# A linear-attention and gated feed-forward kernel: instruction order from a list schedule made at build time, weights transposed by DMA at the start, five banks instead of three for keys, queries and values

## The chip, the cores and the metric

The kernel runs on one core of one Trainium2 chip. The metric is the device time of one execution in microseconds (us). The kernel before takes 217.75 us, the median of its runs. Executions of one kernel differ by about 1%, and some fall into a slower state. Spans quoted from a profile are those of the one execution that was profiled (216.6 us for the kernel before), which is a little shorter than the timed median.

## The reference

One token matrix x (2048 tokens, 512 channels) is layer-normed once. The normed tokens xn feed an attention with 32 heads of 16 channels without a softmax over tokens, and a gated feed-forward block of width 1376; x and both results are added.

```python
xn = layernorm(x)                                   # 2048 x 512
q, k, v = split(xn @ wqkv)                          # 32 heads of 16
pq, pk = q @ w_phi, k @ w_phi                       # per head, 16 x 16
phi_q = concat(softmax(pq), softmax(-pq))           # over 16 features
phi_k = concat(softmax(pk), softmax(-pk))
kv  = einsum("sf,sd->fd", phi_k, v)                 # summed over ALL tokens
num = phi_q @ kv;  den = phi_q @ sum_s(phi_k) + 1e-6
att = (num / den) @ wo
ffn = (gelu(xn @ w_gate) * (xn @ w_up)) @ w_down
out = x + att + ffn
```

Two things matter for the order of work. The attention of any token needs kv, the sum over all 16 token tiles of 128, so all keys and values come before the first attention output. The feed-forward block needs only xn and its weights.

## The kernel before

The weight w_phi is folded into the key and query weights at the start ("fold", 16 small matmuls each), so a key tile is one product of four 512-column matmuls, followed by two exponentials on ScalarE (for +pk and -pk) and four additions on GpSimd, which sum each group of 16 features. Products are written to banks: buffers that each hold one product until other engines have read it. A value tile is one product; VectorE scales it by the reciprocals of the key sums (`vs`), and TensorE accumulates keys times scaled values (`kv_acc`). The feed-forward stage begins when keys and queries are done.

Every instruction stands in the queue of its engine in the order in which the program was written by hand. A helper only adds the semaphore waits. The order of VectorE and GpSimd is therefore fixed by such code:

```python
def ln_rstd(t, n):                                   # VectorE adds, GpSimd takes the power -0.5
    op("dve", ... tensor_scalar(vpe, mv[.., 1], 1e-5, None, op0=ALU.add))
    op("pool", ... tensor_tensor(rstd, vpe, neghalf, op=ALU.pow))

def xt_dma(t):                                       # a normed tile is transposed by a DMA of SyncE
    dma("sp", ... dma_start_transpose(xnT[:, :, t * P:(t + 1) * P], xn_sb[:, t % NXN, :]))

# ---- start: x tile by tile on SyncE's queue, weights on ScalarE's queue, wq transposed by DMA, wk by TensorE
dma("act", ... wk_nat, A_wqkv[:, 512:1024]);  load_x(1)
dma("act", ... wv_sb,  A_wqkv[:, 1024:1536])
...
dma("sp",  ... dma_start_transpose(wqT, A_wqkv[:, 0:512]))
...
# 16 transposes of wk on TensorE, two copies (ScalarE, VectorE), then the folds, then:
for t in range(4, 8): ln_stats(t)
ln_rstd(4, 4)
proj_k(0, 0); proj_k(1, 1)
for t in range(4, 8): ln_norm(t); xt_dma(t)
proj_k(2, 0)
v_recip(0); v_scale(0, 4)                            # values 0 are scaled only here
...
# ---- middle: 28 units (12 keys, 16 queries) in two banks; values always in bank 4
for u, un in enumerate(units):
    b = u % 2
    ...                                              # layer norms of later tiles at fixed units
    if un[0] == "k": proj_k(un[1], b)
    else:            proj_q(un[1], un[2], b)
    ...
    if u % 3 == 2 and nbig < 5:                      # one big weight load every third unit
        big_loads(nbig); nbig += 1                   # wg, wu, wo, wd, tail of wd: on GpSimd's queue
```

The five big loads bring the weights of the later stage (1376, 1376, 512, 1280 and 96 KB). They are issued by GpSimd. They pass the issue points only when GpSimd gets there, because they stand in its queue between the key sums.

The softmax here doesn't subtract the row's maximum and nothing guards it: scores larger than these inputs give would overflow.

## Time and profile before

| quantity, kernel before | us |
|---|---|
| median time | 217.75 |
| span of the profiled execution | 216.6 |
| first key product starts | 14.54 |
| TensorE waits for scaled values, two waits | 6.6 |
| first gate/up product starts | 66.46 |
| from there to 213.50: TensorE busy | 145.26 of 147.04 |

The page of a profile shows in its second part the busy share of each engine in 40 equal slices of the span: each digit is tenths, 9 meaning 90% or more. PEclk is the clock granted to TensorE, in tenths of full speed. These lines are from the page of the kernel before; one slice is 5.4 us.

```profile
span 216.6 us, 3003 instructions
...
PE   7776399949999999999999999999999999998994
...
PEclk9999969997999999999999999999999999999999
...
```

TensorE is at 9 tenths from the tenth slice on, and nearly without a gap from 66 us on. What can be gained lies before that: the first four slices show 6 and 7 tenths, the fifth 3 and the ninth 4. The next lines are from the view of waits of TensorE: the engine and the line that waited, what it waited for, then total us, number of waits, and the longest.

```profile
...
PE ps_all L444 <- DVE vs L428: 6.6, 2, 3.5
...
PE ps_all L562 <- ACT y_sb L580: 0.8, 1, 0.8
...
```

L444 is the accumulation, L428 the scaling of a value tile on VectorE. The two waits end at 26.96 and at 46.94 us. The chain of waits of 6 to 30 us (start, duration, what) shows what stands before the first of them:

```profile
...
16.10 1.03 POOL rstd L345
17.15 2.89 DVE xn_sb L351 x4
20.04 0.48 DVE vs L422
20.55 1.23 DVE vs L428
21.77 0.61 DVE stats L336
...
25.18 0.48 DVE vs L422
25.68 1.24 DVE vs L428
26.96 0.76 PE ps_all L444 x8
...
```

The wait that ends at 26.96 us is for value tile 1. Its product was long done, and GpSimd had the key sums that its scaling needs ready at 22.71 us, but VectorE first takes the statistics of four other tiles (to 24.97 us). Before the second wait VectorE stands still for 2.6 us, for the rstd that GpSimd computes behind key sums. Just after each of the two waits, of 3.5 and 3.0 us, the granted clock falls to half for 3.4 us (from 27.36 and from 47.84 us), and matmuls run at half speed.

One more view: the timeline of GpSimd, cut to its issues of the five big loads (start, duration, line, tiles).

```profile
...
34.71 0.97 POOL L670 DMA_DIRECT2D wg_sb<-in_B_w_gate_dram  x1
...
38.48 0.77 POOL L673 DMA_DIRECT2D wu_sb<-in_B_w_up_dram  x1
...
45.80 0.78 POOL L676 DMA_DIRECT2D wo_sb<-in_A_wo_dram  x1
...
49.36 0.98 POOL L679 DMA_DIRECT2D wd_sb<-in_B_w_down_dram  x1
...
55.88 0.55 POOL L683 DMA_DIRECT2D wd_sb<-in_B_w_down_dram  x1
...
```

The transposes of xn tiles by DMA take 2.4 to 2.5 us to land when no load is in flight; the six that meet one or two loads take 3.2, 4.5, 2.5, 5.0, 3.0 and 6.5 us.

### The profile page before, as it was taken

The page shows a single profiled execution, that of the slowest core. Times are in us where ns is not written, and L with a number is a line of the kernel's source. Part 1 is how long each engine was busy: PE and PEld are TensorE (multiplying, and loading weights), DVE is VectorE, ACT ScalarE, POOL GpSimd, SP SyncE. Part 2 cuts the span into 40 slices and gives each one's busy share as a digit, 9 for nine tenths or more (in the row PEclk, how much of TensorE's full clock was granted, in tenths as well). Part 3 has the DMA queues.
Part 4 walks back from the last instruction along what each step waited for, and adds up shares of the span by engine and source line. Part 5 has one row for each costly group of instructions (what it writes and reads, how often), then busy time and mean ns, then how long its engine had stood idle before and what let it go on. Part 6 is the DMA issues. An engine that isn't in the chain of part 4 may idle for free.

```text
span 216.6 us, 3003 instructions
## 1 busy us (share of the span) xinstructions
PE 199.5 (92%) x1094; PEld 98.3 (45%) x1115; DVE 134.0 (62%) x302; ACT 75.8 (35%) x133; POOL 83.9 (39%) x114
## 2 busy tenths in 40 slices
PE   7776399949999999999999999999999999998994
PEld 2433154424444554554444455544455444543441
DVE  4698988593335877799459575494744777622121
ACT  2449537836886222232312313232232231422000
POOL 3219999999994000022424124323323222440200
PEclk9999969997999999999999999999999999999999
DMA  6892216969300000002020112101140111110101
GB/s 155 250 267 61 49 24 109 390 203 229 123 0 3 0 0 0 3 0 48 24 52 25 24 48 50 26 24 24 48 51 0 50 48 27 48 24 24 47 29 48
DMA packets 24590, 14.40 MB, mean 66 GB/s; under 512 B 18464, under 2 KB 23584, under 8 KB 24576
## 3 DMA queue, kind: packets, MB, share of 16 engines
q1 hardware_dynamic: 21920, 8.39, 17.0%
q0 software_dynamic: 1072, 4.75, 6.6%
q10 hardware_dynamic: 1584, 1.07, 1.8%
q8 instruction: 9, 0.15, 0.3%
q14 instruction: 5, 0.04, 0.1%
HBM read 7.91 MB, written 2.10 MB: 46 GB/s over the span
## 4 chain that ended last, share of the span: by engine, by line
PE 78%; DVE 13%; DMA 3%; POOL 2%; issue 2%; ACT 1%; ACTq 0%; DVEq 0%
PE ps_all L472 32%; PE ps_all L567 18%; PE ps_all L562 6%; PE ps_all L399 5%; PE ps_all L412 5%; PE ps_all L375 4%; PE ps_all L493 4%; PE ps_all L444 4%; DVE stats L336 3%; DMA hT<-in_A_wqkv_dram 3%; DVE xn_sb L351 2%; DVE vs L428 2%; POOL rstd L345 1%; DVE otmp L539 1%; DVE mv L338 1%
## 5 line engine op out<-in xcount | busy, mean ns | idle before, releaser
L485 DVE TENSOR_TENSOR hT<-gs,ps_all 128x512 bf16<-128x512 bf16 (+1 forms) x44 | 30.1, 683 | 31.9 <-PE ps_all L493 23.2
L482 ACT ACTIVATE gs<-ps_all 128x512 bf16<-128x512 f32 (+1 forms) x44 | 26.2, 597 | 57.0 <-PE ps_all L472 47.0
L472 PE MATMUL ps_all<-xnT,wg_sb 128*128 128x512 bf16 (+1 forms) x175 | 45.1, 379 | 0.1
L472 PE MATMUL ps_all<-xnT,wu_sb 128*128 128x512 bf16 (+1 forms) x170 | 44.5, 379 | 0.3
L567 PE MATMUL ps_all<-wd_sb,hT 128*128 128x512 bf16 (+1 forms) x171 | 40.4, 379 | 0.3
L551 POOL TENSOR_TENSOR o_sb<-otmp 128x512 bf16<-128x512 bf16 x16 | 18.4, 1152 | 54.6 <-DVE otmp L539 54.6
L582 POOL TENSOR_TENSOR ob<-y_sb,x_all 128x512 bf16<-128x512 f32 x12 | 13.8, 1153 | 47.3 <-ACT y_sb L580 47.3
L428 DVE TENSOR_TENSOR vs<-ps_all,vs 128x1024 bf16<-128x1024 f32 x16 | 19.6, 1227 | 14.2 <-PE ps_all L412 14.1
L472 PEld LDWEIGHTS ps_all<-xnT,wu_sb 128*128 128x128 bf16 (+1 forms) x176 | 17.6, 100 | 20.4
L567 PEld LDWEIGHTS ps_all<-wd_sb,hT 128*128 128x128 bf16 (+1 forms) x176 | 17.2, 98 | 20.8
L472 PEld LDWEIGHTS ps_all<-xnT,wg_sb 128*128 128x128 bf16 (+1 forms) x176 | 17.0, 100 | 16.6
L380 ACT ACTIVATE Ek<-ps_all 128x512 bf16<-128x512 f32 x32 | 17.2, 597 | 14.5 <-PE ps_all L375 14.4
L580 ACT ACTIVATE y_sb<-ps_all 128x512 f32<-128x512 f32 x12 | 7.2, 597 | 41.7 <-PE ps_all L567 41.7
L539 DVE TENSOR_TENSOR otmp<-ps_all,cf 128x384 bf16<-128x384 f32 (+1 forms) x48 | 21.5, 504 | 0.0
L388 POOL TENSOR_TENSOR st<-Ek 128x512 f32<-128x512 bf16 x16 | 18.6, 1160 | 0.1
L406 ACT ACTIVATE EqT<-ps_all 128x512 bf16<-128x512 f32 x32 | 17.2, 605 | 2.5 <-PE ps_all L399 2.3
L375 PE MATMUL ps_all<-wk,xnT 128*128 128x512 bf16 x61 | 17.0, 405 | 0.6 <-ACT Ek L380 0.3
L399 PE MATMUL ps_all<-xnT,wq 128*128 128x512 bf16 x63 | 17.3, 402 | 0.1
L412 PE MATMUL ps_all<-wv_sb,xnT 128*128 128x512 bf16 x61 | 16.2, 387 | 0.7 <-DMA wv_sb<-in_A_wqkv_dram 0.6
L444 PE MATMUL ps_all<-vs,Ek 128*128 128x136 bf16 x128 | 10.8, 230 | 6.6 <-DVE vs L428 6.6
L562 PE MATMUL ps_all<-wo_sb,oT 128*128 128x512 bf16 x62 | 16.0, 379 | 0.8 <-ACT y_sb L580 0.8
L351 DVE TENSOR_SCALAR xn_sb<-x_all,mv,rstd 128x512 bf16<-128x512 bf16 x16 | 12.1, 797 | 4.8 <-POOL rstd L345 4.8
(56 smaller groups left out, 171.9 us busy)
## 6 DMA issues: line engine op xcount, KB each, us to landing
x_all<-in_A_x_dram SPq DMA_DIRECT2D x16, 128.0 KB, 3.1
out_dram<-ob SPq DMA_DIRECT2D x16, 128.0 KB, 1.7
wg_sb<-in_B_w_gate_dram POOLq DMA_DIRECT2D x1, 1376.0 KB, 7.3
wu_sb<-in_B_w_up_dram POOLq DMA_DIRECT2D x1, 1376.0 KB, 7.3
wd_sb<-in_B_w_down_dram POOLq DMA_DIRECT2D x1, 1280.0 KB, 7.6
hT<-in_A_wqkv_dram ACTq DMA_DIRECT2D x1, 512.0 KB, 5.8
wv_sb<-in_A_wqkv_dram ACTq DMA_DIRECT2D x1, 512.0 KB, 7.1
wo_sb<-in_A_wo_dram POOLq DMA_DIRECT2D x1, 512.0 KB, 4.8
```

The lines of the kernel that those rows point to most:

```text
L375: h = op("pe", lambda e, i=i, t=t, b=b: e.matmul(bank(b), xnT[:, i, t * P:(t + 1) * P], wk2[:, i, :], start=(i == 0), stop=(i == 3)), read ...
L388: op("pool", lambda e: e.tensor_tensor(v1, ev[:, :, 0:8], ev[:, :, 8:16], op=ALU.add), reads=[B_Ek[t]], writes=[B_st[0]])
L399: h = op("pe", lambda e, i=i, p=p, s=s, b=b: e.matmul(bank(b), wq2[:, i, p * 128:(p + 1) * 128], xnT[:, i, s * 512:(s + 1) * 512], start=( ...
L412: h = op("pe", lambda e, i=i, t=t, b=b: e.matmul(bank(b), xnT[:, i, t * P:(t + 1) * P], wv_sb[:, i, :], start=(i == 0), stop=(i == 3)), re ...
L428: h = op("dve", lambda e, v=v, b=b: e.tensor_tensor(v[:, :, :, 0:DH], bank(b).rearrange("p (h d) -> p h d", d=DH).unsqueeze(1).to_broadcas ...
L444: h = op("pe", lambda e, t=t, i=i, sig=sig, p=p, b=b, st=st: e.matmul(bank(b)[:, (i % 3) * GV:(i % 3 + 1) * GV], Ek[:, t, sig, p * 128:(p ...
L472: h = op("pe", lambda e, i=i, s=s, jf=jf, w=w, wt=wt, b=b: e.matmul(bank(b)[0:w, :], wt[:, i, jf * 128:jf * 128 + w], xnT[:, i, s * 512:(s ...
L482: op("act", lambda e, w=w, k=k, J=J: e.activation(gs[0:w, k, :], bank(J % 2)[0:w, :], ACTF.Gelu_apprx_tanh), reads=[BK[J % 2]], writes=[B_ ...
L485: h = op("dve", lambda e, w=w, k=k, J=J, s=s, jf=jf: e.tensor_tensor(hT[0:w, s % 2, jf, :], gs[0:w, k, :], bank(2 + J % 2)[0:w, :], op=ALU ...
L539: op("dve", lambda e, q=q, n=n: e.tensor_tensor(otmp[:, k, q * 384:q * 384 + n * 128].rearrange("p (s h d) -> p s h d", s=n, d=DH), bank(4 ...
L562: h = op("pe", lambda e, j=j, t=t, b=b: e.matmul(bank(b), oT[:, t % NOT, j, :], wo_sb[:, j, :], start=(j == 0), stop=False), reads=[B_oT[t ...
L567: h = op("pe", lambda e, jf=jf, w=w, s=s, tl=tl, b=b: e.matmul(bank(b), hT[0:w, s % 2, jf, tl * 128:(tl + 1) * 128], wd_sb[0:w, jf, :], st ...
```

## The change

The intent: every operation is given a cost, and DMAs a latency, from a table; a list schedule runs over the dependency graph at build time and sets the order of each engine's queue, so that an instruction that is ready is not put behind one that is not. Both weights are transposed by DMA at the start, which takes 16 transposes and two copies away from TensorE, ScalarE and VectorE. Keys and queries take turns in three banks, values in two. The big loads become eligible with keys 4 to 8 instead of every third unit.

```diff
+    def schedule(self):                       # new: list schedule at build time
+        while len(order) < len(self.ops):
+            # the engine that can start earliest; on it, of the ready operations,
+            # the one with the lowest prio (prio = place in the program, unless given)
+            h = min((x for x in cand[n] if x.ready <= t + 1e-9), key=lambda x: x.prio)
+            free[n] = t + h.cost
+            h.end = t + h.cost + h.lat
...
-        dma("act", ... wk_nat, A_wqkv[:, 512:1024])
-        dma("sp", ... dma_start_transpose(wqT, A_wqkv[:, 0:512]))       # after x tile 7
-        for t in range(NT): load_x(t)                                   # on SyncE's queue
+        dma("sp", ... dma_start_transpose(wkT, A_wqkv[:, 512:1024]), cost=4.4, lat=2.4, prio=-900)
+        dma("sp", ... dma_start_transpose(wqT, A_wqkv[:, 0:512]),    cost=4.4, lat=2.4, prio=-900)
+        load_x(0, 1, 2.1); load_x(1, 1, 2.2)                            # on ScalarE's queue
+        dma("act", ... wv_sb, A_wqkv[:, 1024:1536], lat=3.8, prio=-900)
+        load_x(2, 1, 3.5); load_x(3, 1, 3.5); load_x(4, 4, 5.0); load_x(8, 8, 8.0)
...
-            op("dve", ... vpe = var + 1e-5)
+            op("pool", ... vpe = var + 1e-5, cost=0.12, prio=-700)
...
+        def kq():                                                       # banks 0, 1, 2
+            turn[0] += 1; return (turn[0] - 1) % 3
...
+        big = [lambda: dma("pool", ... wg_sb ..., cost=1.0, lat=8.0,
+                           extra=exps[-1:], prio=-500), ...]            # wu, wo, wd, tail alike
+        for s in range(NST):
+            if s < NST - 1: ln_group(4 * s + 4)
+            for m in range(4):
+                proj_k(4 * s + m, kq())
+                if big and s > 0: big.pop(0)()                          # keys 4, 5, 6, 7, 8
+                if m % 2 == 1 or nv < 4: val()                          # values in banks 3, 4
+            ...
+            for m in range(4): proj_q(s, m, kq())
```

`extra=exps[-1:]` ties a load to the exponentials of its key, and `prio=-500` lets it go ahead of all ordinary work of GpSimd once they are done.

## The prediction

> **What bounds it now.** From 66.5 us, the first gate/up product, to 213.5, TensorE is busy 145.3 of 147.0 us (table of stretches). The loss lies before. In the chain of waits eight 512-column matmuls take 1.73 us (0.216 each). By then 168 such are done (16 keys, 16 queries, 10 values: 36.3 us), nine accumulations of 0.47 us (4.2) and about 4.3 us of transposes and folds: 45 us of work, so 21.5 lost. My split:
> - 5.9 us before the first useful matmul;
> - 6.6 us in two waits of the accumulation for VectorE's scaled values (waits of TensorE: 3.5 and 3.0 us). Instruction order is behind them: values 0, whose product was done at 10 us, are scaled at 20.5, behind layer norms; the last rstd stands behind key sums on GpSimd;
> - about 3.8 us after these waits, where matmuls take 0.43 us: granted clock 0.74 in 25 to 30 us. The Trainium skill (TensorE: Matmul & The Clock Gate, HAM clock gate) says an idle window of about 3.4 us halves the clock; this trace agrees, with waits of 3.0 and 3.5 us;
> - about 5 us between 6 and 20 us: key 0 starts at 14.5, behind values, layer norms, the weight's 16 transposes (1.07 us) and two copies (1.02, 0.69).
>
> **The change.** Removed: those transposes, the copies, a 512 KB plain load. Added: a second weight transpose by DMA; the first took 4.9 us to land next to x loads. Moved: x to ScalarE's queue (seven issues of about 0.5 us), rstd's addition to GpSimd (0.17 us off VectorE each). Order follows readiness; a third key/query bank and a second value bank let products run ahead of exponentials (two are 1.09 us against 0.86 of product) and of VectorE (1.8 us per value tile).
>
> **On the path.** Key 0 should start at about 10 us (folds at 7.6). Limits up to the feed-forward start: VectorE 16 x 0.85 (statistics) + 16 x 0.80 (normalise) + 10 x 1.78 (values) + 2 = 46 us, from 3 on; ScalarE 64 x 0.6 + folds from 10 on, about 49; TensorE 43 from 6 on, about 49. I add 4 to 7 us of waits, because the cost table has normalise at 0.42 us where the trace has 0.80 on average (0.40 to 1.25; the skill, SBUF — State Buffer, Who interferes with whom, has VectorE and GpSimd lock a shared port; the spread agrees). Feed-forward then starts at about 56 us, 10 earlier. Afterwards about 0.7 us: the 0.78 us wait for bank 7 at 199.6 goes, as another output tile can be taken first. The attention chain on VectorE (3.2 us), now unbroken, may give some back.
>
> Predicted: 207.0 us, 202.0 to 212.5 in 8 of 10. Faster by over 2%: 0.88; within 2%: 0.09; slower: 0.03.
>
> **Right if** gate/up starts at 54 to 58 us; waits for scaled values fall from 6.6 to under 2 us; mean clock is over 0.99; key 0 starts by 11 us; the later stage stays at 146 to 148 us. **Wrong by step if** key 0 starts after 13 us (DMA transposes delay x or the values' weight), the clock still dips below 0.9 between 20 and 50 us, or the later stage exceeds 149 us.
>
> **What would make it wrong.** Transposes of both weights fill the DMA engines and hold back tiles 0 to 3; earlier weight loads collide with later tiles' transposes; a static order from wrong costs puts a late instruction ahead of a ready one; VectorE bursts stall the up bank.

## The result, and the profile after

The kernel after takes 224.72 us (223.99 to 226.38, four runs). The ratio to the kernel before is 1.033, with a 95% interval of 1.027 to 1.039: slower by over 2%. A ratio here is always the mean time of one kernel's fast runs over the mean of the other's fast runs of the same rounds, so it is not quite the ratio of the medians quoted.

The page of the kernel after; one slice is 5.6 us:

```profile
span 222.9 us, 2963 instructions
...
PE   7487799333999999999999999999999999999993
...
PEclk9769999965699999999999999999999999999999
...
```

Three slices of 3 tenths, between 39 and 56 us, were not there before, and the clock falls in the last two of them and in the one after. The view of waits of TensorE:

```profile
...
PE ps_all L379 <- DMA xnT<-xn_sb: 11.3, 2, 6.1
PE ps_all L371 <- DVE xn_sb L358: 3.2, 2, 2.1
...
PE ps_all L436 <- DVE vs L421: 0.6, 2, 0.4
```

L436 is the accumulation again: its waits for scaled values have gone from 6.6 to 0.6 us, as the change intended. In their place stand 11.3 us in which keys (L379) wait for transposed tiles. The chain of waits, from 30 to 60 us, says which DMA:

```profile
...
31.11 1.23 DVE vs L421
32.34 2.86 DVE xn_sb L358 x4
35.20 0.03 DVE mv L345
35.23 18.57 DMA xnT<-xn_sb
...
53.94 1.86 PE ps_all L379 x4
55.80 0.91 PE ps_all L436 x8
56.71 1.71 PE ps_all L411 x4
58.42 1.58 PE ps_all L379 x4
...
```

A transpose of one tile of 128 KB needed 18.57 us from issue to landing. After it, a product takes 1.86, 1.71 or 1.58 us where it takes 0.86 at full clock, and an accumulation 0.91 where it takes 0.47: the four pieces sum to 6.06 us instead of 3.05, so the half clock costs another 3.0 us. The table of stretches gives, for each stretch, its length and the busy us of PE, PEld, DVE, ACT and POOL with the number of instructions, then the granted clock, the DMA share and GB/s:

```profile
...
40.00:44.00 4.00, 0.81 (x4) 0.20 (x2) 1.50 (x3) 2.40 (x5) 3.66 (x7) 1.00 0.97 211
44.00:48.00 4.00, 1.12 (x3) 0.43 (x4) 1.20 (x3) 0.00 (x0) 3.75 (x8) 0.76 1.02 348
48.00:52.00 4.00, 0.74 (x2) 0.00 (x0) 3.07 (x4) 1.08 (x2) 3.69 (x6) 0.50 1.18 278
52.00:56.00 4.00, 2.06 (x8) 0.99 (x9) 0.00 (x0) 0.16 (x1) 3.61 (x7) 0.50 1.15 186
...
```

In 40 to 56 us TensorE works 4.7 of 16 us while the DMA engines are never idle (a share of 0.97 to 1.18; packets that overlap are counted twice), at 186 to 348 GB/s. What fills them are the five big loads. The timeline of GpSimd, cut to its issues of them:

```profile
...
33.00 0.85 POOL L598 DMA_DIRECT2D wg_sb<-in_B_w_gate_dram  x1 [1.19 <-ACT Ek L383]
...
34.98 0.78 POOL L601 DMA_DIRECT2D wu_sb<-in_B_w_up_dram  x1
36.19 0.75 POOL L604 DMA_DIRECT2D wo_sb<-in_A_wo_dram  x1 [0.44 <-ACT Ek L383]
...
39.09 1.02 POOL L607 DMA_DIRECT2D wd_sb<-in_B_w_down_dram  x1
...
44.07 0.58 POOL L610 DMA_DIRECT2D wd_sb<-in_B_w_down_dram  x1
...
```

They start within 11 us instead of 21. They now land after 9.8, 12.9, 13.3, 14.7 and 10.1 us instead of 7.3, 7.3, 4.8, 7.6 and 2.2. The transposes of the eight tiles 8 to 15, in flight at the same time, take 4.4, 12.8, 18.6, 17.8, 11.8, 6.2, 5.2 and 2.7 us. The view of the tile xnT ends with the time of all twelve transposes:

```profile
...
DMA to landing us min/median/max: 2.5/4.8/18.6
```

The start went wrong too. Key 0 starts at 15.85 us, later than the 14.54 before. x tiles 1, 2 and 3 take 4.4, 6.3 and 7.9 us to land, where the cost table has 2.2 to 3.5; beside them two weight transposes (6.0 and 12.1 us to land), the values' weight (6.3) and the rest of x are in flight. The timeline of VectorE shows what a static order makes of it (in brackets: idle time before, and what ended it):

```profile
...
8.51 0.69 DVE L343 BATCH_NORM_STATS2 stats<-x_all 128x6 f32<-128x512 bf16 x1 [1.71 <-DMA x_all<-in_A_x_dram]
9.24 0.18 DVE L345 BATCH_NORM_AGGREGATE mv<-stats 128x2 f32<-128x6 f32 x1
10.99 0.69 DVE L343 BATCH_NORM_STATS2 stats<-x_all 128x6 f32<-128x512 bf16 x1 [1.56 <-DMA x_all<-in_A_x_dram]
11.60 0.72 DVE L358 TENSOR_SCALAR xn_sb<-x_all,mv,rstd 128x512 bf16<-128x512 bf16 x2
...
```

The first two lines are the statistics of tile 2. The rstd of tile 1 was ready on GpSimd at 8.58 us, so tile 1 could have been normalised after them, at 9.42. Its normalisation stands in the queue behind the statistics of tile 3, because the table said that this tile would be there by then; those statistics wait for their DMA until 10.99 us, and the normalisation starts at 11.60.

The later stage, by contrast, improved. From its first product at 77.35 to 219.55 us it takes 142.20 us, of which TensorE is busy 142.06. Two value products (0.864 us each) and two accumulations (0.47 each) more than before are already done when it begins, 2.67 us of work. At equal work it would be 144.9 us against 147.0 before, 2.2 us faster: the wait for the output bank (0.8 us) is gone, TensorE's weight loads no longer wait for scaled values (1.3 us before), and they wait 0.7 us for attention outputs instead of 2.3.

The balance of the two spans is then: start of the later stage later by 10.9 us, less 2.67 us of work already done, less 2.2 us in the later stage, plus 0.25 us at the end: 6.3 us, which is 222.9 less 216.6.

### The profile page after: what moved, and what is told of

Its sections match the earlier page's. It is cut to its first block, busy times and chain, and to the rows that moved or that the text cites. A ratio compares the mean times of both kernels' runs of the same rounds, so it can differ in the third digit from the quotient of the medians.

```text
span 222.9 us, 2963 instructions
## 1 busy us (share of the span) xinstructions
PE 200.1 (90%) x1099; PEld 99.2 (45%) x1099; DVE 130.3 (58%) x295; ACT 74.4 (33%) x132; POOL 87.4 (39%) x123
## 3 DMA queue, kind: packets, MB, share of 16 engines
q10 hardware_dynamic: 2672, 2.62, 4.0%
## 4 chain that ended last, share of the span: by engine, by line
PE 75%; DMA 12%; POOL 5%; DVE 4%; ACTq 1%; issue 1%; ACT 0%
PE ps_all L462 33%; PE ps_all L536 17%; DMA xnT<-xn_sb 8%; PE ps_all L532 6%; PE ps_all L411 5%; PE ps_all L484 4%; DMA x_all<-in_A_x_dram 4%; PE ps_all L379 3%; PE ps_all L400 3%; PE ps_all L436 3%; POOL st L390 2%; DVE xn_sb L358 1%; POOL st L392 1%; POOL st L394 1%; ACTq L309 1%
## 5 line engine op out<-in xcount | busy, mean ns | idle before, releaser
L462 PE MATMUL ps_all<-xnT,wu_sb 128*128 128x512 bf16 (+1 forms) x176 | 45.2, 379 | 0.0
L468 DVE TENSOR_TENSOR hT<-gs,ps_all 128x512 bf16<-128x512 bf16 (+1 forms) x44 | 29.0, 680 | 27.4 <-PE ps_all L462 27.3
L379 PE MATMUL ps_all<-wk,xnT 128*128 128x512 bf16 x64 | 17.9, 423 | 11.3 <-DMA xnT<-xn_sb 11.3
L406 ACT ACTIVATE EqT<-ps_all 128x512 bf16<-128x512 f32 x32 | 16.6, 612 | 7.7 <-PE ps_all L400 7.7
L411 PE MATMUL ps_all<-wv_sb,xnT 128*128 128x512 bf16 x64 | 18.3, 413 | 0.8 <-DMA wv_sb<-in_A_wqkv_dram 0.8
L400 PE MATMUL ps_all<-xnT,wq 128*128 128x512 bf16 x64 | 15.1, 379 | 1.1 <-ACT wq L557 1.1
L379 PEld LDWEIGHTS ps_all<-wk,xnT 128*128 128x128 bf16 x64 | 6.4, 105 | 20.2 <-issue 14.8
L501 DVE RECIPROCAL r_sb<-ps_all 128x48 f32<-128x48 f32 (+1 forms) x32 | 9.3, 327 | 10.3 <-PE ps_all L484 10.1
## 6 DMA issues: line engine op xcount, KB each, us to landing
wu_sb<-in_B_w_up_dram POOLq DMA_DIRECT2D x1, 1376.0 KB, 12.9
wd_sb<-in_B_w_down_dram POOLq DMA_DIRECT2D x1, 1280.0 KB, 14.7
x_all<-in_A_x_dram ACTq DMA_DIRECT2D x1, 1024.0 KB, 11.8
```

What stands on the lines that cost most here:

```text
L379: op("pe", [lambda e, i=i: e.matmul(bank(b), xnT[:, i, t * P:(t + 1) * P], wk2[:, i, :], start=(i == 0), stop=(i == 3)) for i in range(4)] ...
L400: op("pe", [lambda e, i=i: e.matmul(bank(b), wq2[:, i, p * 128:(p + 1) * 128], xnT[:, i, s * 512:(s + 1) * 512], start=(i == 0), stop=(i = ...
L411: op("pe", [lambda e, i=i: e.matmul(bank(b), xnT[:, i, t * P:(t + 1) * P], wv_sb[:, i, :], start=(i == 0), stop=(i == 3)) for i in range(4 ...
L462: op("pe", [lambda e, i=i, wt=wt, b=b: e.matmul(bank(b)[0:w, :], wt[:, i, jf * 128:jf * 128 + w], xnT[:, i, s * 512:(s + 1) * 512], start= ...
L468: op("dve", lambda e: e.tensor_tensor(hT[0:w, s % 2, jf, :], gs[0:w, k, :], bank(ub)[0:w, :], op=ALU.mult), reads=[B_gs[k], BK[ub]], write ...
```

## The experiments

The leading theory (A) was that the big loads, issued close together, hold the transposes of later tiles back, and that this alone turns a gain into a loss: without the 11.3 us of waits and the 3.0 us of half clock, 224.7 us would be 210.4. The rivals put the loss to the late start, to a static order that is wrong in the middle as well, or to GpSimd being kept from its work. All kernels gave correct results. Runs 1 to 4 shared a chip and the runs of the kernel before (median 217.57), as did 5 to 8 (217.21), 9 to 12 (216.38) and 13 to 15 (217.59).

### Round 1: take one suspect away at a time

**loads_sp.** The loads go to SyncE's queue and wait for the landing of the last transpose.

```diff
-            lambda: dma("pool", ... wg_sb, ..., cost=1.0, lat=8.0, extra=exps[-1:], prio=-500),   # and the other four
+            lambda: dma("sp",   ... wg_sb, ..., cost=0.5, lat=8.0, extra=[last_xt[0]], prio=-500),
...
+            if s == 2:
+                while big: big.pop(0)()
             for m in range(4):
                 proj_k(4 * s + m, kq())
-                if big and s > 0: big.pop(0)()
```

> Only edit to the changed kernel: the five big weight loads go to SyncE's queue and each waits until the last transpose of a normalised tile has landed. Theory A (the loads, issued between 33 and 44 us, starve the transposes of tiles 9 to 15, which took 12 to 19 us to land instead of 2.5): the transposes land in 2.4 to 3 us, the two waits of the key product (11.3 us) and the slow clock behind them (about 3.8 us) go, and the time falls by about 15 us from 224.7 to 208 to 211. Rival B (the list-scheduled orders or the bank split are what idles TensorE, and the transposes are late because they are issued late): the key product still waits over 6 us in total and the time stays above 220.

Measured: 210.18 us (209.52 to 211.09), ratio 0.967 [0.962, 0.972]. The end of its view of the tile xnT, to be held against 18.6 above:

```profile
...
DMA to landing us min/median/max: 2.4/2.5/4.4
```

No key waits for a transpose any more. Key 0 still starts late, at 16.84 us. The time is close to the 210.4 us worked out above: theory A holds. That the size fits so exactly is partly chance: key 0 starts 1.0 us later here than in the kernel after, and round 3 shows that about a fifth of the gain comes with the other queue and engine. The late start cannot be what made the change slower, since this kernel has it and is faster than before by 3.3%.

**loads_late.** Only the point of issue moves, from keys 4 to 8 to keys 8 to 12; queue and engine stay.

```diff
-                if big and s > 0:
+                if big and s > 1:
```

> Only edit to the changed kernel: the five big weight loads stay on GpSimd's queue but are tied to the exponentials of keys 8 to 12 instead of keys 4 to 8. Theory A: tiles 8 to 11 land in 2.5 us as none of the loads is in flight yet, tiles 12 to 15 still meet the first two loads and take 5 to 10 us; the waits of the key product shrink from 11.3 to 2 to 6 us, the time is 211 to 216. Rival B: no change, above 220.

Measured: 219.73 us (219.38 to 222.10), ratio 1.014 [1.006, 1.022]. This missed the expectation. The waits for transposes fell from 11.3 only to 6.2 us, and transposes still took up to 15.0 us. A shift by four keys is not enough, because the last four transposes are still to come then.

**start_lats.** Nothing but the numbers of the cost table: the landing times at the start as the profile after shows them.

```diff
-   wkT: cost=4.4, lat=2.4   wqT: cost=4.4, lat=2.4   x: 2.1, 2.2, 3.5, 3.5, 5.0, 8.0   wv: 3.8   wphi: 3.0
+   wkT: cost=1.4, lat=4.6   wqT: cost=5.8, lat=6.3   x: 2.3, 3.9, 5.8, 7.5, 8.6, 11.4  wv: 5.8   wphi: 4.2
```

> Only edit to the changed kernel: the scheduler's table is told the landing times that the trace shows for the first loads (tile 1 4.3 us, tile 3 7.9, values' weight 6.3, the key weight's transpose 6.0, and so on); the instructions themselves are the same. Theory C (part of the loss is a static order from wrong latencies: VectorE holds the normalise of tile 1 behind tile 3's statistics, and TensorE holds the folds behind the transposes of tile 1): key 0 starts at 12.5 to 14 us instead of 15.8, and the time falls by 1 to 3 us, 221.5 to 224, while the waits for the transposes stay. If the order does not matter at the start: key 0 stays at 15.8 and the time within 0.5 us of 224.7.

Measured: 223.83 us (221.88 to 224.55), ratio 1.028 [1.021, 1.035]. Key 0 starts at 11.00 us, 4.9 us earlier, and the kernel gains less than 1 us (the intervals of the two ratios overlap). The waits for transposes grew to 12.6 us, the longest from 6.1 to 8.9. What is gained at the start is swallowed in the middle as long as the loads collide there.

**wq_later.** The transpose of the query weight waits for x tile 3.

```diff
+        dma("sp", ... dma_start_transpose(wqT, A_wqkv[:, 0:512]), ..., extra=[B_x[3].last_write], prio=-900)   # moved below load_x(3)
```

> Only edit to the changed kernel: the query weight's DMA transpose waits until tile 3 of x has landed. Theory D (the two weight transposes fill the DMA engines and hold the first x tiles back): tile 3 lands at 8 to 9 us instead of 11.0, tile 1 and the values' weight 1 us or so earlier too; key 0 starts at 13 to 14.5 us instead of 15.8; the time falls by 1 to 2.5 us to 222 to 224. If the x tiles are late for another reason (their own queue's order), landing and time do not change.

Measured: 219.78 us (219.65 to 222.72), ratio 1.014 [1.006, 1.022]. Tile 3 lands after 5.3 us instead of 7.9, and key 0 starts at 12.72. The waits for transposes stayed at 11.3 us. The gain of about 5 us is larger than expected, and larger than the 3.1 us by which key 0 comes earlier; I have not traced the rest. In the traces the first gate/up product starts 5.0 us earlier (72.34), the half clock in the middle lasts 10.2 us instead of 13.7, and TensorE waits 0.6 us less in all between key 0 and gate/up; these pieces are not tested. The run does show that the second weight transpose crowds the start.

### Round 2: both repairs together, and what is left for the schedule

**sp_lats.** loads_sp and start_lats together.

> The kernel with the loads behind the last transpose, plus the table of true landing times for the first loads (the two edits that were tried alone). In the loads run GpSimd is busy with key sums from 18.9 us to 68 us almost without a gap, so the start of key 0 (16.8 us there) sets the end of the prologue. If that reading is right, key 0 at about 11 us brings about 5 us: 204 to 207 us. If the gain at the start is swallowed again, as it was with the loads in the way (key 0 at 11.0 us, yet only about 1 us gained): 209 to 211.

Measured: 206.67 us (206.58 to 208.92), ratio 0.956 [0.949, 0.962]: the lowest median of all (sp_lats_norm in round 4, ratio 0.953, is not told apart from it). Its page, of an execution of 207.2 us in which key 0 came at 13.44 us (the three others had spans of 204.8 to 205.0):

```profile
span 207.2 us, 2961 instructions
...
PE   7587899999999999999999999999999999999994
...
PEclk9789699999999999999999999999999999999999
...
```

From the sixth slice to the last but one TensorE is at 9 tenths. In 25 to 63 us it is busy 37.70 of 38 us. The later stage starts at 63.16 us with three values and three accumulations more done than before, 4.0 us of work: at equal work that is 59 us in the profiled execution, and about 57 in the faster ones (an estimate: their spans are 2.4 us shorter, and they were not profiled). The 207.0 us of the prediction are reached once the two faults are mended, and its 56 us nearly.

**sp_lats_wq.** The same with the query transpose of wq_later, and the table set for it.

> The same, plus the query weight's transpose after tile 3 of x, with its own landing times in the table. Alone, that edit brought about 5 us, because VectorE no longer stood still for tile 3. With the order already right, little is left: within 1 us of the run without it, 203.5 to 207. If crowding of the DMA engines at the start costs by itself, another 2 us or more go.

Measured: 207.39 us (206.87 to 211.42), ratio 0.956 [0.951, 0.961]. Nothing further is gained when the table knows the true landing times.

**sp_banks.** loads_sp with the old banks: two for keys and queries, one for values.

```diff
-            return (turn[0] - 1) % 3
+            return (turn[0] - 1) % 2
...
-                proj_v(nv, 3 + nv % 2 if nv < NVK else 4)
+                proj_v(nv, 4)
```

> The kernel with the loads behind the last transpose, but with the banks as before the change: two for keys and queries, one for values. If GpSimd's key sums set the pace of the prologue, the extra banks bring little: 210 to 212 us. If the extra banks are what lets TensorE run ahead: 213 us or more, with waits of key and query products for exponentials.

Measured: 211.44 us (209.71 to 214.09), ratio 0.972 [0.966, 0.979], against 210.18 us and 0.967 [0.962, 0.972] for loads_sp. It was run at another time. The difference is about 1.2 us and the intervals overlap. The three banks are worth little; that they are worth anything is not shown.

**before_sp.** The kernel before, with its loads on SyncE's queue after its last transpose.

```diff
-                dma("pool", ... wg_sb ...)                            # and the other four
+                dma("sp", ... wg_sb ..., extra=[B_xnT[15].last_write])
...
-            if u % 3 == 2 and nbig < 5:
-                big_loads(nbig); nbig += 1
+            if u == 13:
+                for nbig in range(5): big_loads(nbig)
```

> The kernel before the change with one edit: its five big loads go to SyncE's queue and wait for the last transpose of a normalised tile. It asks how much of the gain of the loads run belongs to the loads (4.1 us of GpSimd's issue time and the traffic) and not to the change. If the list schedule and banks carry the gain: 216 to 218 us, as before. If the loads alone do: 210 to 213. My guess is between: 213 to 216, because GpSimd's delay stands behind the second wait of 3.0 us.

Measured: 214.73 us (214.61 to 215.15), ratio 0.991 [0.986, 0.996]. The same repair is worth 2 to 2.5 us in the old order, where waits for scaled values fell from 6.6 to 5.0 us. Against this kernel sp_lats, of the same chip and rounds, stands at 0.9555 / 0.9907 = 0.964. So about 8 of the some 10 us that sp_lats gains are the schedule's and the rest of the change's, not the moved loads'.

### Round 3: place, queue and order

**loads_pool_late.** loads_sp, but the loads stay with GpSimd: `dma("pool", ...)`, each with `extra=[last_xt[0]]`.

> The changed kernel with the loads left on GpSimd's queue, but each waiting for the landing of the last transpose of a normalised tile: the placement of the loads run with the queue of the change. If placement is what counts: no waits for transposes, 210 to 214 us (up to 4 us of GpSimd's issue time come on top of the 210.2 of the run on SyncE's queue, as its key sums set the pace). If the queue is what counts: above 218.

Measured: 212.30 us (211.41 to 213.72), ratio 0.982 [0.976, 0.987]. Transposes take 2.4 to 4.1 us. The ratios are the better measure: the place of the loads alone, with the same engine issuing, brings 1.033 to 0.982, and moving the issue to SyncE as well brings it to 0.967. About four fifths of the repair is the place. The rest came with the move to SyncE's queue, which also spares GpSimd about 4 us of issuing for the five loads in all; that this time is the cause was not tried by itself.

**loads_act.** The reverse: the points of issue stay, ScalarE issues. (Not shown: ScalarE's queue gets 12 semaphores for landings instead of 7, here and in lats_act, as it carries five more DMAs.)

```diff
-            lambda: dma("pool", ... wg_sb, ..., cost=1.0, lat=8.0, extra=exps[-1:], prio=-500),   # and the other four
+            lambda: dma("act",  ... wg_sb, ..., cost=0.5, lat=8.0, extra=exps[-1:], prio=-500),
```

> The changed kernel with one edit: the five big loads are issued from ScalarE's hardware queue instead of GpSimd's software queue, tied to the same exponentials of keys 4 to 8, so they come at about the same time among the transposes. If what starves the transposes is simply that several big loads are in flight (theory A as it stands): transposes of tiles 9 to 13 still take over 8 us, the key product waits 7 us or more in total, 219 to 225 us. If the software queue (or GpSimd's lost issue time) is what did it: transposes land in under 5 us and the time is 208 to 213.

Measured: 215.09 us (213.80 to 218.42), ratio 0.991 [0.986, 0.996]. This lies between the two forecasts. I had expected no repair from another queue (theory A as it stood), and was wrong. The eight transposes took 5.4, 10.4, 12.1, 13.0, 8.4, 9.5, 10.2 and 9.4 us, longer than alone but never 18, and TensorE waited only 2.4 us for them. The profiled execution was in the slow state, with key 0 at 18.02 us, 2.2 us later than in the kernel after, so the place of the loads against the transposes was not quite the same; round 4 repeats it on a better base.

**order_off.** sp_lats, with every engine's queue in the order of the program text.

```diff
+        order = self.ops
+        for n_, h in enumerate(order): h.end = float(n_)
         self._emit(order)
```

> The kernel with loads behind the transposes and the true landing times (206.7 us), with the list schedule switched off: every engine gets its instructions in the order in which the program writes them. It shows how much the schedule itself does. The program text asks for the accumulation right after each key, so TensorE would wait for GpSimd's sums (2.8 us) and VectorE (1.8 us) after most keys: 230 to 260 us, with the accumulation's wait for scaled values the largest. If hand order hardly matters with these banks: below 215.

Measured: 277.49 us (275.97 to 278.25), ratio 1.281 [1.274, 1.288], more than expected. Waits of TensorE:

```profile
...
PE ps_all L441 <- DVE vs L426: 49.1, 16, 8.3
...
```

L441 is the accumulation. The list schedule is not a refinement of a good program order here: the new program text is written to be sorted, and without the sorting the waits for scaled values come back more than sevenfold (49.1 us against 6.6).

**before_bunch.** The kernel before, with its five loads in five consecutive units.

```diff
-            if u % 3 == 2 and nbig < 5:
+            if u >= 2 and nbig < 5:
```

> The kernel before the change with one edit: its five loads are issued in five consecutive units instead of every third, as tightly as in the changed kernel. If bunching as such starves the transposes: those of tiles 12 to 15 land in 6 us or more instead of 2.5 to 6.5. Whether it costs time depends on slack: before, key products alternate with query products and reach tiles 12 to 15 only after 56 us, so I expect 217 to 220 us; above 222 if there is no slack.

Measured: 219.83 us (219.71 to 221.53), ratio 1.018 [1.012, 1.023]. Bunching the loads costs the old kernel about 3.5 us, but not by way of the transposes: these took 6.1 us at most. TensorE's waits for scaled values rose from 6.6 to 8.8 us. Waits of VectorE between 30 and 50 us:

```profile
...
DVE xn_sb L351 <- POOL rstd L345: 5.1, 2, 4.4
...
```

The same wait was 3.3 us (longest 2.6) in the kernel before. GpSimd issues the last load from 43.52 to 44.08 us and starts the awaited rstd at 44.08. That the issue and the sums before it delayed the rstd is read from this timeline; no run changed it alone.

### Round 4: queue or number in flight

loads_act had contradicted the reading that only the place of the loads counts. This round was run on start_lats, whose start is known, to tell the queue from the number of loads in flight.

**lats_act.** start_lats, with the loads issued by ScalarE as in loads_act.

> The kernel with the true landing times at the start (223.8 us, key product waiting 12.6 us for transposes), with one edit: the five loads are issued from ScalarE's hardware queue instead of GpSimd's software queue, at the same exponentials. It separates two readings of the ScalarE run (215.1 us, transposes still 8 to 13 us, but only 2.4 us of waits). If loads on a hardware queue leave the transposes a larger share: landing 5 to 13 us instead of 14 to 19, waits of the key product under 6 us, 210 to 216 us. If that run waited little only because its start was 4 us late in the profile: waits 9 us or more here, and 218 to 223 us.

Measured: 212.77 us (211.82 to 214.24), ratio 0.979 [0.972, 0.986], against 223.83 us for start_lats. It was run at another time. The first four loads go out at 29.8, 31.4, 32.9 and 34.4 us here, at 30.3, 31.2, 33.0 and 37.0 in start_lats: no looser. From the view of waits and the end of the view of the tile xnT, first of start_lats:

```profile
...
PE ps_all L379 <- DMA xnT<-xn_sb: 12.6, 2, 8.9
...
DMA to landing us min/median/max: 2.4/6.0/18.6
```

and of lats_act:

```profile
...
PE ps_all L379 <- DMA xnT<-xn_sb: 3.2, 1, 3.2
...
DMA to landing us min/median/max: 2.4/6.9/11.9
```

The wait for transposes is 3.2 us instead of 12.6. With the same loads at nearly the same times, the queue that carries them, with the engine that issues on it, decides 11 us. GpSimd is also spared the issuing, but 9.4 of the 11 us are the shorter wait itself.

**lats_paced.** start_lats, still on GpSimd's queue, with a load only at every second key.

```diff
-                if big and s > 0:
+                if big and s > 0 and m % 2 == 0:
```

> The same kernel (223.8 us), loads still on GpSimd's queue, but issued after every second key instead of every key (keys 4, 6, 8, 10, 12), about as far apart as before the change. If the number of loads in flight together sets the delay: transposes land in at most 9 us instead of 18.6, waits of the key product fall from 12.6 to 3 to 8 us, 213 to 219 us. If the first two loads are enough to starve the transposes of tiles 8 to 11: still over 14 us and 220 us or more.

Measured: 213.95 us (213.30 to 218.74), ratio 0.982 [0.974, 0.990]. Loads go out at 30.8, 33.6, 41.8, 49.6 and 58.3 us. The transposes:

```profile
...
DMA to landing us min/median/max: 2.4/4.7/8.3
```

The wait is 4.3 us. So on the same queue the spacing decides about 10 us. At most two loads are in flight at a time here, up to three in start_lats; but the last two are now also issued after the last transpose, so number and place are not told apart. Both queue and spacing matter: several loads at once on GpSimd's queue are what starves the transposes.

**sp_lats_norm.** sp_lats with the cost of the normalisation in the table set from 0.42 to its mean in the trace of the kernel before.

```diff
-               reads=[B_x[t], B_mv[t], B_rstd[t]], writes=[B_xn[k]], cost=0.42)
+               reads=[B_x[t], B_mv[t], B_rstd[t]], writes=[B_xn[k]], cost=0.8)
```

> The best kernel so far (206.7 us) with one number in the cost table set to what the trace shows: normalise at 0.80 us instead of 0.42. The prediction took that wrong cost for the reason of 4 to 7 us of leftover waits. If it is: 204 us or less. If the order hardly depends on it: 206 to 208 us.

Measured: 207.67 us (206.53 to 210.06), ratio 0.953 [0.945, 0.961], against 0.956 [0.949, 0.962] for sp_lats. The wrong cost made no difference. The prediction had put 4 to 7 us of waits down to it.

## Why the prediction was wrong

**The step that failed.** The prediction listed, among what would make it wrong, that "earlier weight loads collide with later tiles' transposes", and put nothing for it in the sum: its only allowance for waits, 4 to 7 us, was put down to the cost of normalising. So gate/up, forecast for about 56 us, started at 77.35. The collision was the largest term: 14.3 us, of which 11.3 us were waits and 3.0 us half clock. Removing it (loads_sp) brings 224.72 to 210.18 us. The data for a better estimate were in the profile before: transposes at 2.4 us alone and up to 6.5 us beside one or two loads, and five loads spread over 21 us that the change would tie to five consecutive keys.

**Key 0 "at about 10 us": 15.85.** The cost table has 2.2, 3.5 and 3.5 us for x tiles 1 to 3, where the trace of the kernel before already had 2.5, 5.2 and 6.6; the prediction named this case as a risk as well (start after 13 us, because transposes delay x). The x tiles took up to 7.9 us, and the static order made from 2.2 to 3.5 us put instructions that were not ready ahead of ready ones. Correct numbers in the table alone give 11.00 us (start_lats); landings still vary, and in the profiled execution of sp_lats, with the same table, x tiles 2 and 3 took 9.4 and 9.1 us and key 0 came at 13.44. In the kernel as changed this gain was swallowed later; on top of loads_sp it is worth 2.5 to 3.5 us (ratio 0.967 to 0.956, medians 210.18 to 206.67).

**Waits for scaled values "under 2 us": right.** They went from 6.6 to 0.6 us, and order_off shows that the list schedule does it: 49.1 us without.

**Clock "over 0.99": wrong, by the same cause.** It was 0.954, with 0.50 granted between 48 and 56 us. The Trainium skill (TensorE: Matmul & The Clock Gate, HAM clock gate) puts the idle window that halves the clock at about 3.4 us; the traces agree in part, with waits of 3.0 and 3.5 us before and two that sum to 11.3 after. But in lats_act a wait of 3.2 us (to 41.47) left the clock full, and in sp_lats the clock is half from 21.86 to 25.27 us, after sparse small matmuls and no wait over 1.1 us. So the length of one wait does not settle it here. From the sixth slice on, where sp_lats has no gap to speak of, its clock is full.

**The later stage "146 to 148 us": better.** 144.9 at equal work, 2.2 us faster instead of 0.7. The wait for bank 7 went, as predicted. The attention chain on VectorE gave nothing back.

**"4 to 7 us of waits, because the cost table has normalise at 0.42": fell.** The spread is as the Trainium skill would have it (SBUF — State Buffer, Who interferes with whom: some VectorE instructions lock GpSimd out or wait for it at a shared port), 0.40 to 1.25 us in the trace before (0.40 twice with GpSimd idle, 1.23 to 1.25 beside the longest of its sums), but correcting the cost changed nothing (sp_lats_norm).

**The banks.** The prediction let a third key/query bank and a second value bank carry part of the gain. They are worth about 1.2 us at most by sp_banks, and not separated from nothing.

**The total.** 207.0 us was predicted and 206.67 is reached by sp_lats. The mechanism and the ceiling, a TensorE that is full, were right; the DMAs that feed it were not costed. That the two numbers agree to 0.3 us is luck: sp_lats also has the loads moved, which brings the kernel before 2 to 2.5 us, its start is 1 to 3 us later than forecast at equal work, and between key 0 and gate/up TensorE waits 2.5 us in all, not the 4 to 7 that were added.

**Still open.** Why GpSimd's queue starves transposes more than ScalarE's. The Trainium skill (DMA: Bandwidth & Descriptors, Queues, rings and completion order) says that each DMA engine takes turns between queues, a packet at a time. That would fit, because packets on GpSimd's queue hold more. From the views of DMA queues (packets, MB, share of 16 engines), first of start_lats, then of lats_act:

```profile
...
q0 software_dynamic: 1104, 4.77, 8.0%
...
q10 hardware_dynamic: 5664, 7.37, 11.4%
...
```

GpSimd's queue (q0) moved 4.3 KB a packet. ScalarE's (q10) had 2672 packets and 2.62 MB in start_lats, so the five loads added 2992 packets and 4.75 MB, 1.6 KB each. No run changed the packets alone, so that their size is the reason is not shown.

## What to carry to other kernels

When a change moves a bulk load, count what is in flight beside each small DMA that someone waits for, and give the wait a number from the slowest such DMA in the trace; bulk loads that are needed late belong behind the last small transfer that is needed soon, and not on GpSimd if that engine or its queue is shared. A static order is only as good as its latencies: take landing times from a trace of the schedule itself (here even those of the kernel before would have been nearer than the table), and look at them again after each change. A faster stretch upstream pays only as far as the next wait, so mend the largest wait first and time the others after it.

## What the Trainium skill lacked or had wrong

- DMA: Bandwidth & Descriptors, Rules for kernel authors, says that "A transpose next to ordinary DMAs needs nothing". That row is about correct results, and all 15 kernels were correct. For time it misleads: one tile's transpose took 2.4 us alone, up to 6.5 us (before) and 8.3 us (lats_paced) beside one or two bulk loads, and 18.6 us with up to four in flight on GpSimd's queue. No page gives this slowdown.
- The same section says of spreading DMAs over issuing engines that it "only saves sequencer issue time". The same five loads at nearly the same times, issued by ScalarE instead of GpSimd, brought the longest transpose from 18.6 to 11.9 us and the time from 223.8 to 212.8 us. The page's advice in SWDGE vs HWDGE vs iDMA, plain loads from SyncE or ScalarE, agrees with the result; the page does not name a neighbour's slower transposes as a reason.
- No page has the landing times of several start-up DMAs together: x tiles of 128 KB landed after 4.4, 6.3 and 7.9 us, and weight transposes of 512 KB after 6.0 and 12.1 us, with all of them in flight.
